# Four places for raw pieces of weights, and a new order of the first part, in a kernel of windowed attention and two products

## The chip, the core and the metric

The program runs on one core of a Trainium2 chip. The engines of a core are called by the names of its profile: PE (TensorE, matrix products; PEld is its loading of weights), DVE (VectorE), ACT (ScalarE), POOL (GpSimd) and SP (SyncE, which issues nearly all DMAs here). Each engine works through a queue of its own in order; semaphores tie the queues together. The metric is the device time of one execution in microseconds (us); lower is better.

## What is computed

The reference, cut to what matters (B = 4, H = 8, S = 768, D = 64; 8 global keys, a window of 96; 3072 tokens, d_model 512, d_ff 2048):

```
scores = q @ k.T / sqrt(D) - slope[h] * dist      # slope[h] = 2 ** -(h + 1)
keep   = key is among the first 8, or 0 <= query - key < 96
a      = softmax(where(keep, scores, -1e9))
x      = (a @ v), heads side by side              # 3072 x 512
h      = x @ w_in                                 # 3072 x 2048
g      = h if h >= 1;  0 if h <= -1;  else (h + 1) ** 2 / 4
out    = g @ w_out                                # 3072 x 512
```

The queries, keys and values are 32-bit floats, the two weights are 64-bit floats. The products have to be nearly as exact as in 32-bit arithmetic.

## The kernel before

*Tiling.* Work is cut into 24 units of 128 queries of one batch, all heads: units 0 to 3 are the first 128 queries of the four batches, units 4 to 23 the rest, batch by batch. Two units make a block `c` of 256 tokens, 0 to 11. Every operand of a large product is split into a high and a low half of 16 bits, and three products of halves (high x high, high x low, low x high) make one of nearly 32 bits.

*The first units* (`first_scores`, `masked`, `expo`, `first_turn`, `first_pt`, `first_av`, `scale_x`, `first_xt`, `first_x`) need only their own 128 keys and are computed in 32 bits, half a unit (four heads, `hf` 0 or 1) at a time. Their bias stands in `own_bias`, which lies over place 7 of the tile `wd`; a `slope` makes the bias of one head. The other units fetch k, q and v (`fetch`, on SP), convert them into halves (`conv_hi` on ACT, `conv_lo` mostly two steps on POOL, L767 and L768), put the 32 global keys ahead of the window (`keep_glob`, `set_glob`), and go through `scores`, `masked`, `expo`, `split_p`, `turn_p`, `attend`, `scale_x`, `split_x`, `turn_x`.

*Weights.* They come in 32 pieces `n` of 512 KB, 0 to 15 of w_in and 16 to 31 of w_out. `w_load` (SP) brings the raw 64-bit pieces into a place of `wd`: place `n % 3`. `w_bits` (DVE, L532, L536, L540; for the pieces marked "s" in `WS` the middle step is one of ACT, followed by `w_sign` on POOL) builds the 32-bit float out of two halves of 32 bits, in another part of `wd`, places 3 to 6. `w_hi` (ACT, L549) and `w_scale` (ACT, L560) make the high half and the scaled piece, and `w_lo` (POOL, L567) the low half. Steps 0 of pieces 5, 7, 9 and so on of w_in use the PSUM tile `spare(1)` ("spare" in the trace), the others a tile of the scores ("w_bits"). A raw place can be loaded again when the last step that reads it is over.

*The two products.* `ffn1(c, g)` (L939) is 24 matmuls for two of the 16 slices of d_ff and needs weight pieces 2g and 2g+1 and all four `x` steps of the block. `gelu(c, g, s)` is the nonlinearity: step 0 on ACT (L958), 1 and 2 on DVE (L962, L964), then, for blocks 0 to 2, step 3 on ACT and step 4 on POOL (L972), which make the halves `ga`. `ffn2(c, t, f)` (L998) is the product with w_out for blocks 0 to 2. For later blocks gelu has ten steps and the second product is done with seven products of sums and differences (`diff`, `first_products`, `last_products`, L1042), whose weight differences are kept in `wd` once its raw places are no longer wanted. `ffn1` has two PSUM tiles (`h`); gelu holds one until its step 2. The results of step 0 stand in one of three tiles `u`.

*Order.* All of this is a plan of 3311 items. The list `PLACE` gives the sequence in which they are emitted, and so the order in each engine's queue; `SLOTS` gives the tile that each takes among its like. Both are written out. Beside the items the list holds 37 fillers (`warm`, L494): matmuls of zeros into `spare(0)`. In the queue of PE the stretch from 30 to 75 us goes in pairs: `ffn1(1,g)`, then `ffn1(0,g')`, as fast as weights arrive. `scores(4)` and `scores(5)` follow near 99 and 105 us, and `ffn2` of block 0 behind them.

Of the kernel before, what the change touches and what calls it, by code (L numbers as in the profile page):

```python
# [24 lines left out]
NFC = DFF // P  # L25
# [256 lines left out]
    "v": [int(n, 16) for n in "012100201201212010201201"],  # L282
    "x": [int(n, 16) for n in "101001010110100110111001101011000110011010010110"],
    "xh": [int(n, 16) for n in "1010100101100110010101011010100110101001"],
    "xt": [int(n, 16) for n in "011010101010"],
    "z": [int(n, 16) for n in "101010101011010101001011001011001100101101001"],
}
NFILL = 200
# [53 lines left out]
def fast_path(ctx, tc, q, k, v, nraw, nval, w_in, w_out, out, half, one, stat, marks, badi):  # L342
# [37 lines left out]
    def after(*keys):  # L380
        assert did.issuperset(keys), keys
# [1101 lines left out]
```

## Time and profile before

| | us |
|---|---|
| median of 3 runs | 594.23 (592.88 to 594.45) |
| the profiled execution | 592.99 |
| its span in the trace | 591.1 |
| PE busy | 571.7 (97%) |
| POOL busy | 502.2 (85%) |
| DVE busy | 473.5 (80%) |
| ACT busy | 440.2 (74%) |

The span runs from the first to the last instruction of the trace; the execution's own time is 1.9 us more. The times of the trace below are microseconds from the start of the span. The granted clock of PE is full in every slice of the page.

### The profile page before, as it was taken

To read this page: it belongs to the slowest core of one execution; us is meant where nothing else is said; L and a number is where in the kernel's file an instruction comes from. 1 tells how busy PE (TensorE), PEld (TensorE's weight loads), DVE (VectorE), ACT (ScalarE), POOL (GpSimd) and SP (SyncE) were. 2 spreads that over 40 slices of the span, in tenths; PEclk is the share of its full clock that TensorE was granted. 3 is DMA by queue.
4 is the path that set the end of the run, shared out by engine and by line. 5 is a ranking of instruction groups with operands and counts; after the bars stand their busy time and mean duration, and the time that the engine had idled before them with its cause. 6 is when DMAs were issued, how large, how long until landed. Compare 5 with 4: busy or idle time off the path is not lost.

```text
span 591.1 us, 16452 instructions
## 1 busy us (share of the span) xinstructions
PE 571.7 (97%) x6243; PEld 475.7 (80%) x6243; DVE 473.5 (80%) x1175; ACT 440.2 (74%) x1146; POOL 502.2 (85%) x570
## 2 busy tenths in 40 slices
PE   7998999899999999999999999999999999999995
PEld 5876764457768688988888889888889889898884
DVE  8998999999884788787987987888979877874321
ACT  5998898998866798776976877868868768635340
POOL 0888999879999999899899998799899799579780
PEclk9999999999999999999999999999999999999999
DMA  7875675694840557848865777767667677250001
GB/s 248 279 247 189 203 238 185 144 173 88 191 105 2 114 129 153 179 127 197 196 160 129 171 176 155 179 172 188 169 150 170 158 172 171 56 123 1 2 37 42
DMA packets 144235, 88.19 MB, mean 149 GB/s; under 512 B 108180, under 2 KB 124820, under 8 KB 144148
## 3 DMA queue, kind: packets, MB, share of 16 engines
q1 hardware_dynamic: 144144, 87.05, 59.1%
q8 instruction: 51, 0.84, 0.6%
q14 instruction: 36, 0.29, 0.2%
q10 hardware_dynamic: 4, 0.00, 0.0%
HBM read 54.53 MB, written 6.29 MB: 103 GB/s over the span
## 4 chain that ended last, share of the span: by engine, by line
PE 66%; DVE 11%; ACT 10%; DMA 5%; POOL 4%; issue 3%; ACTq 0%; SPq 0%; DVEq 0%; POOLq 0%
PE h L939 30%; PE o L1042 26%; ACT z L644 5%; PE s L813 4%; PE av L854 4%; PE o L998 3%; DMA wd<-in_moe_w_out_dram 2%; DMA wd<-in_moe_w_in_dram 2%; DVE wd L540 2%; DVE u L964 1%; DVE h L962 1%; ACT ph L827 1%; POOL ga L972 1%; DVE w_bits L536 1%; DVE ph L829 1%
## 5 line engine op out<-in xcount | busy, mean ns | idle before, releaser
L939 PE MATMUL h<-xt,wih 128*128 128x256 f16 x1536 | 256.0, 273 | 5.0 <-DVE u L964 4.9
L939 PE MATMUL h<-xt,wil 128*128 128x256 f16 x768 | 209.3, 273 | 0.0
L939 PEld LDWEIGHTS <-wih 128*128 128x128 f16 x1536 | 148.4, 98 | 29.2 <-DVE u L964 9.9
L962 DVE SCALAR_TENSOR_TENSOR h<-h,u 128x512 f32<-128x512 f32 x96 | 66.4, 692 | 42.1 <-ACT u L958 41.6
L644 ACT ACTIVATE z<-z,stat 128x256 f32<-128x256 f32 (+1 forms) x192 | 91.5, 479 | 9.2 <-DVE stat L632 9.1
L983 POOL TENSOR_TENSOR ga<-u,ga 128x512 f16<-128x512 f32 x72 | 88.3, 1227 | 10.1 <-ACT ga L981 9.8
L1042 PEld LDWEIGHTS <-ga 128*128 128x128 f16 x864 | 83.2, 98 | 10.0
L958 ACT ACTIVATE u<-h,half 128x512 f32<-128x512 f32 x96 | 65.1, 678 | 33.0 <-PE h L939 22.6
L939 PEld LDWEIGHTS <-wil 128*128 128x128 f16 x768 | 75.2, 98 | 8.7
L974 POOL TENSOR_TENSOR u<-u 128x256 f32<-128x256 f32 x72 | 60.2, 838 | 20.0 <-DVE u L964 18.9
L988 POOL TENSOR_TENSOR gb<-u,gb 128x384 f16<-128x384 f32 x72 | 72.0, 1002 | 3.7 <-ACT gb L986 3.7
L1042 PE MATMUL o<-wd,ga 128*128 128x256 f16 x432 | 70.7, 273 | 0.0
L1042 PE MATMUL o<-woh,ga 128*128 128x256 f16 x288 | 70.7, 273 | 0.0
L1042 PEld LDWEIGHTS <-gb 128*128 128x128 f16 x648 | 62.3, 98 | 8.4 <-issue 1.0
L981 ACT ACTIVATE ga<-u 128x512 f16<-128x512 f32 x72 | 44.4, 621 | 33.2 <-POOL u L976 26.6
L964 DVE SCALAR_TENSOR_TENSOR u<-u,h 128x512 f32<-128x512 f32 x96 | 65.2, 680 | 3.6
L829 DVE SCALAR_TENSOR_TENSOR ph<-z,ph 128x1024 f16<-128x1024 f32 x40 | 57.0, 1428 | 9.4 <-ACT ph L827 9.0
L632 DVE CUSTOM_DVE_ANT_0 z<-s,bias 128x256 f32<-128x256 f32 x160 | 59.1, 414 | 5.1 <-PE s L813 4.7
L998 PE MATMUL o<-woh,ga 128*128 128x512 f16 x192 | 61.4, 379 | 0.6 <-ACT ob L1115 0.6
L1042 PE MATMUL o<-wd,gb 128*128 128x256 f16 x432 | 60.6, 273 | 0.8 <-DVE ob L1093 0.8
L998 PEld LDWEIGHTS <-ga 128*128 128x128 f16 x288 | 27.3, 98 | 30.6 <-issue 2.2
L599 DVE TENSOR_REDUCE stat<-c_raw 128x1 f32<-128x256 f32 x128 | 48.5, 406 | 4.3 <-DMA c_raw<-in_moe_w_in_dram 4.3
(132 smaller groups left out, 1172.2 us busy)
## 6 DMA issues: line engine op xcount, KB each, us to landing
wd<-in_moe_w_in_dram SPq DMA_DIRECT2D x16, 512.0 KB, 4.5
wd<-in_moe_w_out_dram SPq DMA_DIRECT2D x16, 512.0 KB, 4.2
c_raw<-in_moe_w_in_dram SPq DMA_DIRECT2D x32, 256.0 KB, 3.0
c_raw<-in_moe_w_out_dram SPq DMA_DIRECT2D x32, 256.0 KB, 3.4
kr<-in_k_dram SPq DMA_DIRECT2D x28, 256.0 KB, 3.6
vr<-in_v_dram SPq DMA_DIRECT2D x28, 256.0 KB, 3.6
qr<-in_q_dram SPq DMA_DIRECT2D x24, 256.0 KB, 3.9
out_dram<-ob SPq DMA_DIRECT2D x23, 256.0 KB, 3.1
```

Of the source, the lines that this page charges most:

```text
L632: nc.vector.tensor_tensor_reduce(out=p32[u, hf][:, hh, :], in0=pts[u, hf][hh // 2][:, hh % 2, 0:n], in1=(own_bias if n == P else bias)[:, ...
L644: nc.scalar.activation(z, z, AF.Exp, bias=nm[:, c : c + 1], scale=-1.0, accum_out=sums[:, c : c + 1])
L829: nc.vector.scalar_tensor_tensor(phs[u, hf][:, 1, :], zf, SP_, phs[u, hf][:, 0, :], op0=ALU.mult, op1=ALU.subtract)
L939: nc.tensor.matmul(hp[:, :, e, :], w[:, dc, f], xt[:, hf, 2 * a + j, :], start=(n == 0), stop=(n == 3 * NDC - 1),)
L958: nc.scalar.activation(u, h, AF.Relu, bias=half, scale=2.0 / (SV * SW), accum_out=su[:, col : col + 1])
L962: nc.vector.scalar_tensor_tensor(h, h, 4.0 / (SV * SW), u, op0=ALU.mult, op1=ALU.max)
L964: nc.vector.scalar_tensor_tensor(u, u, 4.0, h, op0=ALU.min, op1=ALU.mult)
L974: nc.gpsimd.tensor_sub(f[:, 3:7:3], f[:, 0:6:5], f[:, 4:5].to_broadcast([P, 2, P]))
L983: nc.gpsimd.tensor_sub(gas[c, g][:, 1], f[:, 0:4], gas[c, g][:, 0])
L988: nc.gpsimd.tensor_sub(gbs[c, g][:, 1, 0:3], f[:, 4:7], gbs[c, g][:, 0, 0:3])
L998: nc.tensor.matmul(po, a, w[:, f, :], start=(f == 0 and n == 0), stop=(f == NFC - 1 and n == 2))
L1042: nc.tensor.matmul(acc[:, e], x, w, start=first and n == 0, stop=last and n == 2)
```

## The change

Three constants are new (`R4`, `GM`, `WL`), the formula of the raw place in `w_load` is another, and `PLACE` and `SLOTS` are written anew. With the values given to `GM` and `WL`, the new branches in `w_lo`, `put_weight` and `gelu` (a gelu by squares, low halves made on DVE) are never taken, so they change nothing.

```
+R4 = 9
+GM = "d"
+WL = "pppppppppppppppppppppppppppppppp"
...
     def w_load(n):
         num, src, hi, lo = piece(n)
-        r = wd[:, n % 3].bitcast(I32).rearrange("p t a b -> p (t a b)")
+        r = wd[:, n % 3 if n < R4 else (7, 0, 1, 2)[(n - R4) % 4]].bitcast(I32).rearrange("p t a b -> p (t a b)")
...
     def w_lo(n):
-        after(("hi", n), ("scale", n))
-        nc.gpsimd.tensor_sub(lo, wf[n], hi)
         did.add(("w", n))
+        if WL[n] == "v":
...
+        else:
+            after(("hi", n), ("scale", n))
+            nc.gpsimd.tensor_sub(lo, wf[n], hi)
...
 PLACE = [
-    0, 2, 1, 10, 13, 8, 20, 11, 4, 29, 3, 5, 6, 7, 89, 90, 91, 31, 15, 21, 16, 19, 18, 14, 38, 30, 39, 43, 34, 41, 26,
...
```

Pieces 0 to 8 keep their places. Piece 9 goes to place 7, piece 10 to place 0, 11 to 1, 12 to 2, 13 to 7 and so on, each four behind the last one in its place; place 7 is that of the first units' bias.

The items are the same but for six fillers more (43). What changes in `PLACE` is their sequence. On each engine the last part of the queue is the same list before and after: the last 371 items of PE, 544 of DVE (from `split_x(10,0,1)`), 418 of ACT and 335 of POOL (from `gelu(4,0,.)`), 160 of SP. Before that, up to about 255 us of the old run, the sequence differs, mostly by a few positions. The queue of DVE from its 95th to its 121st step, old and new:

```
 95 gelu(0,1,1)          w_bits(9,0)
 96 w_bits(9,0)          w_bits(10,0)
 97 first_x(3,1,1)       first_x(3,1,1)
 98 w_bits(9,1)          w_bits(9,1)
 99 gelu(0,1,2)          gelu(0,1,1)
100 w_bits(9,2)          w_bits(9,2)
101 w_bits(10,0)         gelu(0,1,2)
102 w_bits(10,1)         w_bits(10,1)
103 w_bits(11,0)         w_bits(11,0)
104 w_bits(10,2)         w_bits(10,2)
105 gelu(1,0,1)          w_bits(12,0)
106 w_bits(11,2)         gelu(1,0,1)
107 gelu(1,0,2)          w_bits(12,1)
108 w_bits(12,0)         gelu(1,0,2)
109 gelu(0,2,1)          w_bits(11,2)
110 w_bits(12,1)         gelu(0,2,1)
111 gelu(0,2,2)          w_bits(12,2)
112 w_bits(13,0)         gelu(0,2,2)
113 w_bits(12,2)         w_bits(13,0)
114 w_bits(13,1)         w_bits(14,0)
115 gelu(1,1,1)          w_bits(13,1)
116 w_bits(13,2)         gelu(1,1,1)
117 gelu(1,1,2)          w_bits(13,2)
118 w_bits(14,0)         gelu(1,1,2)
119 gelu(0,3,1)          w_bits(14,2)
120 w_bits(14,2)         w_bits(16,0)
```

On SP the loads of pieces keep about their sequence among the fetches (`w_load(14)` and `w_load(16)` move ahead of a fetch, `fetch(4,"v",0)` moves back from the 25th to the 41st item). On POOL three `conv_lo` of units 4 and 5 move ahead of steps of weights. In the middle, the steps of blocks 1 and 2 and of units 6 to 9 are put in another sequence on all engines.

## Rows read from the trace of the kernel before

**Rows 1.** The page, part 1: busy time of an engine, share, instructions.

```profile
PE 571.7 (97%) x6243; PEld 475.7 (80%) x6243; DVE 473.5 (80%) x1175; ACT 440.2 (74%) x1146; POOL 502.2 (85%) x570
```

**Rows 2.** Windows: stretch, its us, engines' busy us (count), PEclk, DMA share, GB/s.

```profile
45.00:60.00 15.00, 12.75 (x106) 9.75 (x104) 13.19 (x23) 13.21 (x30) 13.16 (x13) 1.00 0.58 180
165.00:180.00 15.00, 15.00 (x140) 11.51 (x139) 11.59 (x18) 7.41 (x18) 14.82 (x16) 1.00 0.26 64
240.00:270.00 30.00, 30.00 (x346) 26.92 (x344) 24.99 (x60) 22.45 (x56) 27.16 (x32) 1.00 0.68 149
```

**Rows 3.** PE's timeline: start us, us, engine, line, operation, out<-in, count, [idle <-releaser].

```profile
37.27 0.38 PE L939 MATMUL h<-xt,wih 128*128 128x256 f16 x2
...
42.52 1.03 PE L494 MATMUL spare<-zeros 128*128 128x512 f16 x4
...
44.29 0.39 PE L939 MATMUL h<-xt,wih 128*128 128x256 f16 x2 [0.75 <-DVE u L964]
...
51.78 0.39 PE L939 MATMUL h<-xt,wih 128*128 128x256 f16 x2 [1.07 <-DVE u L964]
...
99.30 1.50 PE L813 MATMUL s<-kh,qh 64*128 64x128 f16 x47 [1.30 <-DVE wd L540]
...
105.43 1.51 PE L813 MATMUL s<-kh,qh 64*128 64x128 f16 x48 [0.53 <-DVE kh L795]
```

**Rows 4.** DVE's timeline, 31 to 97 us, columns as in the group before.

```profile
31.15 0.68 DVE L540 SCALAR_TENSOR_TENSOR wd<-wd,w_bits 128x512 int32<-128x512 int32 x1
...
36.39 0.68 DVE L532 TENSOR_SCALAR spare<-wd 128x512 int32<-128x512 int32 x1
...
39.80 0.70 DVE L532 TENSOR_SCALAR w_bits<-wd 128x512 int32<-128x512 int32 x1 [0.58 <-DMA wd<-in_moe_w_in_dram]
...
43.55 0.68 DVE L964 SCALAR_TENSOR_TENSOR u<-u,h 128x512 f32<-128x512 f32 x1
...
44.73 0.70 DVE L532 TENSOR_SCALAR w_bits<-wd 128x512 int32<-128x512 int32 x1 [0.50 <-DMA wd<-in_moe_w_in_dram]
...
48.05 0.69 DVE L532 TENSOR_SCALAR spare<-wd 128x512 int32<-128x512 int32 x1 [0.84 <-DMA wd<-in_moe_w_in_dram]
...
48.65 0.68 DVE L540 SCALAR_TENSOR_TENSOR wd<-wd,w_bits 128x512 int32<-128x512 int32 x1
...
96.17 0.69 DVE L532 TENSOR_SCALAR w_bits<-wd 128x512 int32<-128x512 int32 x1 [0.68 <-DMA wd<-in_moe_w_out_dram]
```

**Rows 5.** The chain of waits in order of time: start us, us, what.

```profile
42.47 5.55 DMA wd<-in_moe_w_in_dram
...
51.15 5.11 DMA wd<-in_moe_w_out_dram
...
168.24 2.62 PE h L939 x24
...
375.29 2.05 ACT z L644 x9
```

**Rows 6.** The page, part 6: DMAs, KB each, median us to landing.

```profile
wd<-in_moe_w_in_dram SPq DMA_DIRECT2D x16, 512.0 KB, 4.5
wd<-in_moe_w_out_dram SPq DMA_DIRECT2D x16, 512.0 KB, 4.2
...
kr<-in_k_dram SPq DMA_DIRECT2D x28, 256.0 KB, 3.6
```

**Rows 7.** POOL's timeline, its first weight step and two conversions.

```profile
15.50 1.16 POOL L567 TENSOR_TENSOR wil<-wd,wih 128x512 f16<-128x512 f32 x1 [14.65 <-ACT wd L560]
...
61.28 0.64 POOL L767 TENSOR_SCALAR kr<-kr 128x512 f32<-128x512 f32 x1
...
63.13 0.61 POOL L767 TENSOR_SCALAR kr<-kr 128x512 f32<-128x512 f32 x1
```

**Rows 8.** Timelines of ACT and of PE in the middle.

```profile
161.79 0.69 ACT L958 ACTIVATE u<-h,half 128x512 f32<-128x512 f32 x1 [2.46 <-POOL ga L972]
...
164.15 0.39 PE L939 MATMUL h<-xt,wih 128*128 128x256 f16 x2 [0.88 <-DVE u L964]
```

More of the change, by code (lines that the diff above doesn't have):

```diff
@@ L107 @@
 PLACE = [
[158 rows of a table removed]
[158 rows of a table added]
 ]
 SLOTS = {
-    "ga": [int(n, 16) for n in "b469a7318025bc4943c798b07251a839bc460ab7130259cb6a5704b6b1873a590642c8304bc7531a29b0652852b7a34c01698564a086b27c456a935b91745082ac7b62b3b715c62a8b490c3498132b6a0749c640"],
-    "h": [int(n, 16) for n in "11011010111010101010101010010101010101001101110101010010010101010110101010010110101010101010110100101010100"],
-    "in": [int(n, 16) for n in "13520432105435124013454021350215423105314352141054212541013012134231524535142052"],
-    "k": [int(n, 16) for n in "201201021020120120120120"],
@@ L272 @@
-    "kg": [int(n, 16) for n in "0000"],
-    "o": [int(n, 16) for n in "101001101010101001100101101001010110010110101"],
-    "ob": [int(n, 16) for n in "02102202001010021202010121100110"],
-    "ph": [int(n, 16) for n in "00011010101001010110101010100101010101011010"],
-    "pt": [int(n, 16) for n in "010110111010100101100101010110011001011001100110"],
-    "q": [int(n, 16) for n in "01010110100101010110"],
-    "r": [int(n, 16) for n in "011010100110110111011001011010100110100101010101"],
-    "raw": [int(n, 16) for n in "1001100110100110101011000110100011010010101100011010010011010100"],
@@ L280 @@
-    "s": [int(n, 16) for n in "0231213102031232131203120313120301233321330103101210120103212301303210331210320213312010201312231003012300102320321001012323213003321001031222012323230112021313210302123031302113021322"],
-    "u": [int(n, 16) for n in "21212012011201211202102100210202120102102011021020102102102102101201202120120120120102102021002021021021"],
-    "v": [int(n, 16) for n in "012100201201212010201201"],
-    "x": [int(n, 16) for n in "101001010110100110111001101011000110011010010110"],
@@ L284 @@
-    "xh": [int(n, 16) for n in "1010100101100110010101011010100110101001"],
-    "xt": [int(n, 16) for n in "011010101010"],
-    "z": [int(n, 16) for n in "101010101011010101001011001011001100101101001"],
+    "ga": [int(n, 16) for n in "74ca5836b019274ab5284a7096b28a5374b0185cb0638745a28b915a6c50b2879a5436593510cb8746a9524c2a307b465891c29359470ac632b1752028c37941a65c817b057421a609a20c3b2a870436c9125a3c"],
+    "h": [int(n, 16) for n in "01010100100101010101010101010101010101010101001010101010000101010101010101101110010101010110110100101001011"],
@@ new lines @@
+    "in": [int(n, 16) for n in "51230154302410352423514302143025150342351430113452101042325145540354234500301453"],
+    "k": [int(n, 16) for n in "201201201202121021021021"],
+    "kg": [int(n, 16) for n in "1111"],
+    "o": [int(n, 16) for n in "101010011010101001010101101010101001101001010"],
+    "ob": [int(n, 16) for n in "02012121010102120110201201101220"],
+    "ph": [int(n, 16) for n in "01111010101010011001011010100101100101100101"],
+    "pt": [int(n, 16) for n in "011011010101100110100110101010011110100110011001"],
@@ new lines @@
+    "q": [int(n, 16) for n in "01010010101010101001"],
+    "r": [int(n, 16) for n in "001111010111100110010110010101011010100110010101"],
+    "raw": [int(n, 16) for n in "1010011001011001011111010100100100101111010010010101010010010010"],
+    "s": [int(n, 16) for n in "3120312013120310230213213020321010323030201202120301212130213201201320113202311230023123023320021313013210312032310201230103310233203132201332130232213031013221123013102323023123032113"],
+    "u": [int(n, 16) for n in "20210102102012021220120212102121012021021200120101210210210120121021020120101201201210210120112120120210"],
@@ L287 @@
+    "v": [int(n, 16) for n in "012202102102102101201210"],
+    "x": [int(n, 16) for n in "111101011101100110011001010110110101101101101000"],
+    "xh": [int(n, 16) for n in "1010011010100110010110100110100101100110"],
+    "xt": [int(n, 16) for n in "100101010101"],
+    "z": [int(n, 16) for n in "101011010101010011001100101011001101010010110"],
 }
@@ L565, in w_lo @@
         num, src, hi, lo = piece(n)
-        after(("hi", n), ("scale", n))
-        nc.gpsimd.tensor_sub(lo, wf[n], hi)
         did.add(("w", n))
+        if WL[n] == "v":
+            after(("hi", n))
+            nc.vector.scalar_tensor_tensor(lo, wf[n], SW, hi, op0=ALU.mult, op1=ALU.subtract)
+        else:
+            after(("hi", n), ("scale", n))
+            nc.gpsimd.tensor_sub(lo, wf[n], hi)
     def put_weight(n, t, tl):
@@ L581, in put_weight @@
         at(t + WO[0], w_hi, n)
-        at(t + WO[1], w_scale, n)
+        if WL[n] != "v":
+            at(t + WO[1], w_scale, n)
         at(t + WO[2], w_lo, n)
@@ L946, in fast_path, with square @@
     gas, gbs = {}, {}
+    def square(c, g):
+        return GM[min(c * (NFC // 2) + g, len(GM) - 1)] == "s"
     def gelu(c, g, s):
-        after(("g", c, g, (None, 0, 1, 2, 3, 4, 4, 6, 5, 8)[s])) if s else None
+        after(("g", c, g, (None, 0, 10 if square(c, g) else 1, 2, 3, 4, 4, 6, 5, 8, 1)[s])) if s else None
         did.add(("g", c, g, s))
@@ L960, in gelu @@
             )
+        elif s == 1 and square(c, g):
+            nc.gpsimd.tensor_scalar(u, u, 4.0, 1.0, op0=ALU.min, op1=ALU.mult)
+        elif s == 10:
+            nc.scalar.activation(u, u, AF.Square)
+        elif s == 2 and square(c, g):
+            nc.vector.scalar_tensor_tensor(u, h, 16.0 / (SV * SW), u, op0=ALU.mult, op1=ALU.max)
         elif s == 1:
@@ L1160, in put_ffn1 @@
             at(t + GEL[s], gelu, c, g, s)
+            if s == 1 and square(c, g):
+                at(t + GEL[1] + 0.6, gelu, c, g, 10)
     def put_ffn2(c, ts, g, t):
```

315 rows, old and new, of the table PLACE are left out of this document.

## The prediction

> **What bounds the kernel now.** I read the page's busy shares first [rows 1]: TensorE (PE) is busy 97% of the 591.1 us span, so only time in which it waits, or works on fillers, can be won. The table of windows [rows 2] splits the run. From 165 us on PE is busy 15.00 us of 15, and the chain of waits [rows 5] is PE alone until 374. Before that PE has gaps; at 45 to 60 us it is down to 12.75 of 15, and VectorE (DVE, 13.19), ScalarE (ACT, 13.21) and GpSimd (POOL, 13.16) are all fuller. The change touches the order up to about 255 us, so the first 165 us decide.
>
> How PE loses there is seen in its timeline [rows 3]. The first-product steps of a pair of blocks, `ffn1(1,g)` and the next `ffn1(0,g')`, are 2.62 us each (24 matmuls, as the chain shows such steps), 5.24 for two. The pairs start at 37.27, 44.29 and 51.78, a fourth of the same kind at 59.41: 7.0, 7.5 and 7.6 us apart. The difference is filled with matmuls of zeros (L494) and a last wait of 0.75, 1.07 and, in the fourth, 1.00 us for DVE's L964, the second gelu step of an earlier `ffn1`, which frees the PSUM tile.
>
> DVE's timeline [rows 4] says what DVE did meanwhile. An operation of weights or gelu starts 0.60 us after the one before it (48.05 to 48.65). From the end of the gelu of (1,0) at 44.2 (L964, from 43.55) to that of (1,1) DVE has 10 of these in the old order, 6.0 us, and two waits for raw weights of 0.50 and 0.84: 7.3, against 7.5 seen. To that of (1,2) it has 11, 6.6 us, and one more such wait, 0.98: 7.6. So DVE sets the pace, and the raw loads add to it. Six such waits stand in its timeline (four of them in rows 4), for pieces 10, 12, 13, 16, 26 and 30: 0.58 + 0.50 + 0.84 + 0.98 + 0.36 + 0.68 = 3.94 us. Behind 97 us PE waits 1.30 at `scores(4)` and 0.53 at `scores(5)` [rows 3]; four more gaps of that kind follow, 0.59 at 107.86 for POOL's last weight, 0.58 at 109.68 for the output tile, and in the middle 0.46 and 0.88, the last in [rows 8].
>
> **Part 1, four places.** A load can be issued when the place's former piece has been read. In the old code that is piece n-3, in the new code, from piece 10 on, n-4. From issue to DVE's start the chain shows four pieces, 5.11 to 5.55 us, mean 5.33 [rows 5]; I take 5.3. A piece costs DVE two or three operations and the gelus between them, about 3.5 us, so the fourth place gives each load some 3.5 us more; that covers the old waits. But the new order uses this room: it takes several pieces earlier. I follow each tight load against the new list, in the old run's times:
> - Piece 10 still goes to place 0 and now needs piece 6 read, 32.3 us (L540 from 31.15 in rows 4, with 0.5 us more work before it). It lands at about 37.5. The new order puts its first step directly behind that of piece 9, at 36.6 (36.39 in rows 4, 0.6 less work ahead, 0.2 for a later start below, 0.60 for piece 9). DVE waits 0.9 where it waited 0.58, and `first_x(3,1,1)`, on which `ffn1(1,0)` depends, is now queued behind that wait: `ffn1(1,0)` comes about 1 us later.
> - Pieces 12 to 14: each lands 0 to 3 us ahead of its step. No wait.
> - Piece 16: its place is free after piece 12's last step, three operations past the gelu of (1,0), 45.1 + 1.8 = 46.9, so it lands at 52.2; DVE is there 11 operations past that gelu, at 51.7. Wait 0.5.
> - Pieces 15 and 18 need a sign step on POOL to be over; they land within 0.5 us of their steps. I put 0.3 for both. Piece 26: none.
> - Piece 30 has eleven short steps between the release (piece 26) and its own, 4.8 us against 5.3: 0.5.
> Sum 2.2, so 1.7 us of 3.94 are won. Bounds: nothing, if all landings are as tight as in the old order, and 3.9.
>
> The trace of before has no four places, and its loads take 5.1 to 5.6 us. The Trainium skill (DMA: Bandwidth & Descriptors, section "Anatomy of one DMA") gives a fit of 2.0 us plus bytes by 436 GB/s, for GpSimd-issued transfers, which would be an estimated 3.2 us for 512 KB. By that the 2.2 us would vanish too. These rows, on SP's queue, do not agree with it, so I don't use it.
>
> SP's queue is in order. Piece 9 now goes to place 7, which holds the first units' bias until `masked(3,1)` is over (near 30 us by its steps); the old issue, behind the read of piece 6, was at 31.9. Behind it stand pieces 10 to 12 and the loads of unit 4.
>
> **Part 2, the order up to the second product.** The same instructions run, so the work of an engine up to a point both orders share is equal, and only idle time can differ. Such a point on DVE is `set_glob(5,k)`: in both lists it is the 206th step, with the same 205 before it, and PE's `scores(5)` at 105.43 waits for it [rows 3]. So what DVE saves in waits, `scores(5)` gains. At the front the new order puts two slopes of bias (0.14 us each) behind the first masks, where DVE waits for PE anyway: no gain; the first exponential stays. ACT has 1.5 us more before piece 0's scaling, so POOL's first weight starts at about 16.9, not 15.5 [rows 7]; its later waits cover that. I charge DVE 0.2 for its start.
>
> Six more fillers (43 for 37) are 6 x 0.216 = 1.3 us (four take 1.03 with a last one of 0.38, rows 3). They stand before `ffn1(1,0)`, `(1,1)` and `(1,3)`, where PE waits for DVE; I cost them nothing. Uncovered they cost up to 1.3.
>
> POOL gets three conversions of units 4 and 5 (L767 and L768) ahead of weights it used to do first. At about 1.85 us each by their starts (61.28, 63.13, rows 7), and with gelus, the work ahead of piece 13's last step grows by 7.7 us, of piece 15's by 1.1, of piece 17's by 4.4. POOL has idled 22.1 us by then in the old run, most of it before its first weight [rows 7]; with the late start and the gaps filled I expect 18.5. Then piece 13 is ready at 65.2 (needed about 68.4), 15 at 69 (71.8), 17 at 75.2 (77.1). So it is covered, by 2 to 3 us.
>
> Sum for `scores(5)`: 1.7 - 0.2 = 1.5 us earlier.
>
> **Part 3, the middle.** PE's 0.88 us at 164.15 goes back to ACT, which waited 2.46 us for a `u` tile until POOL's `gelu(2,3,4)` was over [rows 8]. In the new POOL order that step stands in front of `gelu(2,2,4)` and a weight-difference step, with 2.3 us less work ahead of it; on DVE 2.4 and on ACT 2.7 us less stand ahead of the gelu of (2,4). The wait falls to near nothing, as does most of the 0.46 at 145. I take 1.1 us. Bounds: 0 (the next `u` tiles, of (2,6) and (2,7), get about 1 us tighter) and 2.5 (the 0.58 and 0.59 us go too).
>
> **Behind 165 us** PE is the chain, and what starts 2.6 us earlier stays so, if POOL follows. POOL is busy 27.2 us of 30 at 240 to 270 [rows 2]; it can.
>
> **Sum:** 1.5 + 1.1 = 2.6 us. The profiled run took 592.99 us, giving 590.4. The median of before is 594.23, 1.24 above that run; 2.6 off it gives 591.6, which I predict.
>
> **Rivals.**
> - *Loads land early.* If landing takes the DMA table's medians, 4.5 and 4.2 us [rows 6], all waits on raw weights go (3.9 - 0.2), and the middle gives 2.0: 594.23 - 5.7 = 588.5. Against: on the chain of this stretch they took over 5.1.
> - *POOL takes DVE's place.* If POOL has idled as much as before by 70 us (22.1), piece 17 is ready at 78.8, 1.7 us after PE wants it, and `u` tiles at 55 to 72 us are freed up to 1 us late. That eats the 1.5 and half of part 3: 593.6. For it: ACT and POOL are both over 13 of 15 busy [rows 2]. Against: most of POOL's gaps were waits for ACT.
> - *The lead is given back later.* At 374 to 412 us the chain leaves PE for ACT, POOL and DVE [rows 5]. If those queues do not move up, 594 again. Against: the chain enters them from PE's scores at 373, so they should shift too.
> - *SP's queue stalls ACT: slower.* The load of unit 4's second k block stands behind pieces 9 and 10 and needs `first_av(3,1)` over. ACT converts it right before `gelu(1,0)`, at 39.2. Issued by 33 it lands (3.6 us, rows 6) at 37 and nobody waits; issued at 35.0, the old end of `first_av(3,1)`, with 5.3 us it lands at 40.3, and ACT, POOL and through the gelu PE wait 1.1 us. From an issue at about 34 on it costs. With piece 10's 1 us before `ffn1(1,0)` and 1.3 us of fillers no longer hidden, and no load wait saved, that is 594.23 + 3.4 - 1.1 = 596.5.
>
> **How the numbers follow.** Forecast 0.40, loads land early 0.18, POOL 0.17, given back 0.08, SP 0.17. Within 0.3%, 1.8 us, is about what a measurement cannot tell from no change. The forecast's own spread (0 to 1.5 us either way) puts 0.28 of its 0.40 beyond that: faster 0.28 + 0.18 + 0.03 = 0.49, within 0.34, slower 0.17. The range leaves out the slower rival's end and the best corner (all loads and all of the middle): 588.3 to 595.3.
>
> **What would show it.** DVE's waits for raw weights at 35 to 97 us: 2.2 us in all, the largest before piece 10. `ffn1(1,0)` about 1 us later than 37.27, `scores(5)` 1.5 us earlier than 105.43. No wait of ACT over 1 us for a `u` tile near 160. The same work behind 255 us, moved up by 2.6 us. I am wrong if POOL's or ACT's waits grow at 39 to 80 us, or if `scores(5)` is early and the end is not.

## The result, and the profile after

The changed kernel is slower: a median of 597.64 us (596.09 to 600.01, 11 runs) beside 594.29 (592.04 to 595.53, 11 runs) for the kernel before on the same chip. The ratio is 1.0068 with an interval of 1.0049 to 1.0086, which is 2.9 to 5.1 us. The profiled execution took 596.09 us, its span is 594.2, so in the traces the difference is 3.1 us (591.1 before).

What the prediction called is mostly there. The first part of the page, answering [rows 1], gives nearly the same busy times, but PE's is 2.6 us more, 1.9 of it in the matmuls of zeros (43 of them, 12.85 us, for 37, 10.94):

```profile
PE 574.3 (97%) x6249; PEld 475.7 (80%) x6249; DVE 471.8 (79%) x1175; ACT 440.3 (74%) x1146; POOL 501.8 (84%) x570
```

The windows of [rows 2] in the trace after (columns as there):

```profile
45.00:60.00 15.00, 14.85 (x116) 10.82 (x115) 14.88 (x26) 13.71 (x31) 14.11 (x14) 1.00 0.73 219
165.00:180.00 15.00, 15.00 (x131) 11.02 (x130) 10.36 (x20) 10.39 (x24) 14.00 (x14) 1.00 0.62 141
240.00:270.00 30.00, 30.00 (x346) 26.82 (x345) 24.20 (x59) 23.05 (x59) 27.65 (x34) 1.00 0.69 155
```

From 45 to 60 us PE is busy 14.85 us for 12.75, DVE 14.88 for 13.19: the waits on raw weights have gone. DVE's timeline has only two left between 28 and 100 us, 1.27 us in all for 3.94 [rows 4]:

```profile
34.77 0.69 DVE L535 TENSOR_SCALAR w_bits<-wd 128x512 int32<-128x512 int32 x1 [0.58 <-DMA wd<-in_moe_w_in_dram]
38.94 0.69 DVE L535 TENSOR_SCALAR w_bits<-wd 128x512 int32<-128x512 int32 x1 [0.69 <-DMA wd<-in_moe_w_in_dram]
```

PE's timeline after, at the steps of [rows 3] and [rows 8] and where it lost time later (L947 is the old L939, L821 the old L813, L982 the old L964, L862 the second product of attention, old L854):

```profile
38.56 0.38 PE L947 MATMUL h<-xt,wih 128*128 128x256 f16 x2
...
103.28 1.51 PE L821 MATMUL s<-kh,qh 64*128 64x128 f16 x48
...
122.37 0.86 PE L862 MATMUL av<-vh,pt 128*128 128x64 f16 x24 [0.51 <-DVE vh L805]
...
142.73 1.51 PE L821 MATMUL s<-kh,qh 64*128 64x128 f16 x48 [0.90 <-DVE kh L803]
...
145.39 0.39 PE L947 MATMUL h<-xt,wih 128*128 128x256 f16 x2 [1.15 <-DVE u L982]
...
162.15 0.38 PE L947 MATMUL h<-xt,wih 128*128 128x256 f16 x2
...
278.52 0.88 PE L862 MATMUL av<-vh,pt 128*128 128x64 f16 x24 [0.73 <-DMA pt<-ph]
...
415.94 0.87 PE L862 MATMUL av<-vh,pt 128*128 128x64 f16 x24 [1.16 <-DMA pt<-ph]
```

To see where the lead went, compare the starts of steps that have the same matmul work ahead of them in both sequences. (`scores(5)` isn't quite such a step: it starts 2.15 us earlier, but one `ffn2` step of 0.65 us has moved from ahead of it to behind it, so its lead is 1.5.)

| step on PE | before | after | after minus before |
|---|---|---|---|
| `ffn1(1,0)` | 37.27 | 38.56 | +1.29 |
| `scores(6)` | 114.30 | 112.34 | -1.96 |
| `scores(8)` | 143.04 | 142.73 | -0.31 |
| `ffn1(2,2)` | 145.01 | 145.39 | +0.38 |
| `ffn1(3,7)` | 206.28 | 206.54 | +0.26 |
| `attend(12,1)` | 277.37 | 278.52 | +1.15 |
| `attend(18,0)` | 411.23 | 412.15 | +0.92 |
| `attend(18,1)` | 413.23 | 415.94 | +2.71 |
| end of the span | 591.1 | 594.2 | +3.1 |

So the lead of the front was spent between 115 and 146 us. By 167 us PE was 0.71 ahead once more, since the wait of 0.88 [rows 8] has gone, and between 180 and 192 us it lost 0.97 again, 0.59 of it in two waits for DVE (0.26 at 182.85 and 0.33 at 189.45); no experiment looks into that. Two more losses came on top, at 277 and at 415 us, in the part whose sequence is the old one. The experiments take these places one by one.

### The profile page after: what moved, and what is told of

Same layout as the page of the kernel before. It is cut to its first block, busy times and chain, and to the rows that moved or that the text cites. A ratio compares the mean times of both kernels' runs of the same rounds, so it can differ in the third digit from the quotient of the medians.

```text
span 594.2 us, 16476 instructions
## 1 busy us (share of the span) xinstructions
PE 574.3 (97%) x6249; PEld 475.7 (80%) x6249; DVE 471.8 (79%) x1175; ACT 440.3 (74%) x1146; POOL 501.8 (84%) x570
## 4 chain that ended last, share of the span: by engine, by line
PE 57%; POOL 14%; ACT 9%; DVE 9%; DMA 5%; issue 4%; SPq 0%; ACTq 0%; POOLq 0%; DVEq 0%
PE h L947 26%; PE o L1060 22%; PE s L821 3%; PE o L1016 3%; ACT z L652 3%; PE av L862 3%; POOL wd L1051 2%; DMA pt<-ph 2%; DMA wd<-in_moe_w_in_dram 2%; POOL ga L990 2%; POOL u L992 1%; POOL ga L1001 1%; ACT ph L835 1%; DVE wd L543 1%; POOL kh L776 1%
## 5 line engine op out<-in xcount | busy, mean ns | idle before, releaser
L947 PE MATMUL h<-xt,wih 128*128 128x256 f16 x1536 | 256.1, 273 | 2.8 <-DVE u L982 1.9
L947 PE MATMUL h<-xt,wil 128*128 128x256 f16 x768 | 209.5, 273 | 0.0
L947 PEld LDWEIGHTS <-wih 128*128 128x128 f16 x1536 | 148.4, 98 | 26.6 <-DVE u L982 5.6
L1001 POOL TENSOR_TENSOR ga<-u,ga 128x512 f16<-128x512 f32 x72 | 85.8, 1193 | 13.6 <-ACT ga L999 13.5
L1060 PEld LDWEIGHTS <-ga 128*128 128x128 f16 x864 | 82.9, 98 | 10.4 <-POOL ga L1001 0.3
L947 PEld LDWEIGHTS <-wil 128*128 128x128 f16 x768 | 75.0, 98 | 9.5 <-issue 0.7
L1006 POOL TENSOR_TENSOR gb<-u,gb 128x384 f16<-128x384 f32 x72 | 73.7, 1027 | 6.6 <-ACT gb L1004 6.5
L982 DVE SCALAR_TENSOR_TENSOR u<-u,h 128x512 f32<-128x512 f32 x96 | 65.0, 679 | 3.5 <-DVE h L980 0.5
L1004 ACT ACTIVATE gb<-u 128x384 f16<-128x384 f32 x72 | 36.5, 514 | 21.6 <-POOL u L996 10.8
```

The source lines that it names most:

```text
L947: nc.tensor.matmul(hp[:, :, e, :], w[:, dc, f], xt[:, hf, 2 * a + j, :], start=(n == 0), stop=(n == 3 * NDC - 1),)
L982: nc.vector.scalar_tensor_tensor(u, u, 4.0, h, op0=ALU.min, op1=ALU.mult)
L1001: nc.gpsimd.tensor_sub(gas[c, g][:, 1], f[:, 0:4], gas[c, g][:, 0])
L1006: nc.gpsimd.tensor_sub(gbs[c, g][:, 1, 0:3], f[:, 4:7], gbs[c, g][:, 0, 0:3])
L1060: nc.tensor.matmul(acc[:, e], x, w, start=first and n == 0, stop=last and n == 2)
```

## The experiments

Below, "lost" is PE's time up to a step less the matmul work ahead of it; it compares traces whose sequences differ. One trace of the same queue is not another to a tenth: in two executions of kernels that have the old queue up to 100 us PE stood 1.0 and 1.1 us ahead of the trace of before by then. Differences of under 1 us between two traces are therefore read beside the medians. The size of the front's lead is such a difference: over all traces, `scores(6)` starts at 113.2 to 114.3 us in the six with the old first part (mean 113.8) and at 112.0 to 113.2 in the nine with the new one and its fillers (mean 112.4). So the lead is real, but 1.4 us is a better figure for it than the 1.96 of the table.

### At 415 us: which tile a load was given

The queue of SP is the same there in both kernels, but `SLOTS["raw"]` is not. It gives each small load of raw weights for the check (`check_load`, into `c_raw`) one of two tiles, and in the new list `check_load(20,1)` gets the tile that the load just before it has filled. SP's queue, before and then after (start us, us of the issue; SPq is SP's sequencer):

```profile
401.92 2.81 SPq L836 DMA_TRANSPOSE pt<-ph  x1
404.84 0.53 SPq L594 DMA_DIRECT2D c_raw<-in_moe_w_out_dram  x1
405.47 2.97 SPq L836 DMA_TRANSPOSE pt<-ph  x1
```

```profile
403.77 0.33 SPq L602 DMA_DIRECT2D c_raw<-in_moe_w_out_dram  x1
404.19 2.91 SPq L844 DMA_TRANSPOSE pt<-ph  x1
409.26 0.33 SPq L602 DMA_DIRECT2D c_raw<-in_moe_w_out_dram  x1
409.69 2.85 SPq L844 DMA_TRANSPOSE pt<-ph  x1
```

Before, the load follows the transpose at once. After, the first transpose is issued by 407.10 and the load stands until 409.26, when DVE has reduced what was in its tile (DVE's `check_reduce` steps run from 408.49). Behind it stands `turn_p(18,1)`, for which `attend(18,1)` waits: the chain of waits after is

```profile
409.69 6.21 DMA pt<-ph
...
415.94 0.87 PE av L862 x24
```

Two runs moved the tiles alone, without a change of any queue. In the first, the changed kernel got the old tiles for these loads, in the second, the kernel before got the new ones from piece 9's check on (both lists differ in more loads than the one above):

```
-    "raw": ... "1010011001011001011111010100100100101111010010010101010010010010"
+    "raw": ... "0101100110100110100100100110100100101101010010011010101100101011"
```

> The kernel after, every queue in its own order; only the two tiles that take the weight checks' loads (c_raw) are dealt out as in the kernel before from check_load(20,1) and check_load(18,1) on, where after gives both a tile that has just been filled. Theory A (the tiles, not the order, cost the time late in the run): the 1.8 us that after loses against before at attend(18,1), near 415 us, and the 0.25 near 500 us are gone: 597.6 - 2.0 = 595.6 us; check_load(18,1) no longer waits for a check_reduce, and PE does not wait before attend(18,1). Theory B (the new order costs the time, the waits near 415 us are only where it shows): 597.6 us.

```
-    "raw": ... "1001100110100110101011000110100011010010101100011010010011010100"
+    "raw": ... "0110100110100110100000101011011011010000101101101010101101101101"
```

> The kernel before, every queue in its own order and with three places; only the two c_raw tiles are dealt out as in after, from check_load(9,1) on (near 310 us). Theory A: the wait of PE before attend(18,1) appears here too and the run takes 594.3 + 2.0 = 596.3 us. Theory B: 594.3 us, as no order is touched.

The changed kernel with the old tiles took 595.51 us, 1.0024 (1.0006 to 1.0041) of before; a second measurement of the changed kernel as it is gave 597.47, 1.0066 (1.0045 to 1.0086):

> The kernel after, unchanged, beside the others of this group. Theory A: ratio to before 1.005 to 1.0065, 3 to 3.9 us, and in its trace again about 1.7 us more lost than before near 415 us (attend(18,1)); the 0.85 us lost near 277 us at attend(12,1) needs no cause in the order and may be absent.

The kernel before with the new tiles took 594.37, 1.0023 (1.0002 to 1.0045): 1.4 us more than before by the ratio, 0.6 by the medians (593.77); less than the 2, with an interval that holds it. SP's queue of the two, first the changed kernel with old tiles, then the old with new tiles:

```profile
406.64 3.12 SPq L844 DMA_TRANSPOSE pt<-ph  x1
409.87 0.51 SPq L602 DMA_DIRECT2D c_raw<-in_moe_w_out_dram  x1
410.48 3.12 SPq L844 DMA_TRANSPOSE pt<-ph  x1
```

```profile
402.23 2.85 SPq L836 DMA_TRANSPOSE pt<-ph  x1
407.29 0.33 SPq L594 DMA_DIRECT2D c_raw<-in_moe_w_out_dram  x1
407.73 3.05 SPq L836 DMA_TRANSPOSE pt<-ph  x1
```

The gap in SP's queue goes with the tile, whatever the order. From `attend(18,0)` to `attend(18,1)`, at equal work, PE takes 1.8, 2.0 and 1.9 us more than before in three traces with the new tile (after, after again, old order with new tiles), and no more than before with the old tiles. So the tile costs about 2 us, by the traces and by the medians of the changed kernel (597.47 to 595.51, ratios 1.0066 and 1.0024), and that is about half of the slowdown.

### The front: does the new order win by itself?

One run took the new order and places up to 128 us only, and the old order and tiles behind; another did the reverse, the old order with three places up to 125 us and the new one from there on, with the old tiles of the check. Each is a `PLACE` spliced out of the two lists.

```
 PLACE = [
-    ...  the sequence after
+    ...  the sequence after up to norm(6,1), then the items left, in the sequence before
```

> Order and places of after up to about norm(6,1), near 128 us, then order and tiles of before. Theory A: at scores(5) to scores(7) after is ahead of before by 1.9 us in the traces, and before's middle and end keep that: 594.3 - 1.9 = 592.4 us. Theory B (the early lead is lost again wherever it meets the shared engines, as POOL and DVE have no room): 594.3 us or more.

```
 PLACE = [
-    ...  the sequence after
+    ...  the sequence before up to about 125 us, then the items left, in the sequence after
```

> Order of before with three places up to about 125 us, then the order of after, with before's c_raw tiles late in the run. Prediction's third part: the wait of 0.88 us before ffn1(2,6) goes and 1.1 us are won: 592.7 us. Theory D (POOL sets the pace in the middle in either order; the new one gives 0.88 back and adds waits of 0.5 at attend(5,0), 0.9 at scores(8), 0.7 more at ffn1(2,2)): no gain, 594 to 595 us.

The early order alone took 594.45 us, 1.0021 (1.0001 to 1.0040): no gain. By its trace it is 1.1 us ahead of before at `scores(7)` (at equal work) and 0.15 ahead from `scores(10)` to `attend(12,0)`, and at 277 us it loses 1.8 us more (below). The new middle alone took 593.78, 1.0012 (0.9992 to 1.0031), and loses 31.6 us in all where before loses 31.5. So the lead isn't eaten by the new middle order: the old one eats it as well. That felled my theory that the front's gain would show once the rest was left as it was.

### Places and order, one without the other

```
-        r = wd[:, n % 3].bitcast(I32).rearrange("p t a b -> p (t a b)")
+        r = wd[:, n % 3 if n < 12 else (7, 0, 1, 2)[(n - 12) % 4]].bitcast(I32).rearrange("p t a b -> p (t a b)")
```

> The kernel before, order and tiles untouched; from piece 12 on raw pieces go to places 7, 0, 1, 2 in turn, so that each may be loaded one piece earlier. The prediction's price list says that DVE's waits for pieces 12 to 30 (0.50 + 0.84 + 0.98 + 0.36 + 0.68 = 3.4 us) go, and that scores(5) comes that much earlier less what another engine holds back: 1 to 3 us. Theory D (POOL sets the pace from 135 to 250 us, and what DVE and PE win before does not reach it): the end moves by at most 0.5 us, 593.8 to 594.3 us.

```
-R4 = 9
+R4 = 99
```

> The kernel after with three places again (piece n in place n % 3); the issue of 17 loads stands a little later in SP's queue, behind the last read of the piece before in the place; the other queues are as in after. If the new order needs the fourth place, DVE waits for raw pieces 3 to 6 us more in all and scores(5) comes 2 to 5 us later than in after (103.3); the end is 599 to 602 us. Theory D: POOL takes up the first part of that delay, the end moves by less than half of what scores(5) loses.

In the second, 17 loads were also moved behind the last read of their place, since three places have no room for them earlier. The old order with four places took 594.29 us, 0.9999 (0.9983 to 1.0014): the place alone gives nothing. The new order with three places took 620.92, 1.0462 (1.0445 to 1.0480), over 18 us worse than I had allowed for: its DVE waits eleven times for raw weights, 23.7 us in all, up to 3.88 at a time, and `scores(5)` comes at about 126 us. The new order lives on the fourth place.

Why the place alone gives nothing is seen in DVE's waits of the first of these kernels, and in its chain:

```profile
41.06 0.70 DVE L532 TENSOR_SCALAR w_bits<-wd 128x512 int32<-128x512 int32 x1 [1.06 <-DMA wd<-in_moe_w_in_dram]
...
43.72 0.69 DVE L532 TENSOR_SCALAR spare<-wd 128x512 int32<-128x512 int32 x1 [1.23 <-DMA wd<-in_moe_w_in_dram]
```

```profile
37.37 6.32 DMA wd<-in_moe_w_in_dram
```

Only these two waits are left in place of six, 2.29 us for 3.94, but they are larger than the old ones: three loads of 512 KB are now in flight together (issued at 35.4, 37.4 and 37.8 us, landed at 41.0, 43.7 and 45.2), and they take 5.7, 6.3 and 7.4 us where the old chain showed 5.1 to 5.6 [rows 5]. A load that is issued earlier into a busy stretch doesn't land earlier by as much. (This profiled execution, 595.07 us, is the slowest of its twelve: PE waits 2.52 us at 46.85 and then runs at a lower clock for 3.4 us.)

### The middle: whose queue has no room

The lead is PE's and DVE's. POOL never had it: up to 150 us POOL is idle 29.7 us in the trace before, 30.0 after and 29.8 with the early order alone; its first weight step, which [rows 7] show at 15.50, starts at 17.39. The early-order kernel's `ffn1(2,6)` waits as in [rows 8], for a `u` tile behind POOL's low half:

```profile
161.64 0.69 ACT L970 ACTIVATE u<-h,half 128x512 f32<-128x512 f32 x1 [2.45 <-POOL ga L990]
```

```profile
164.00 0.39 PE L947 MATMUL h<-xt,wih 128*128 128x256 f16 x2 [0.89 <-DVE u L982]
```

To see whether POOL sets the end there, POOL does one step of 1.16 us (`gelu(2,1,4)`) twice, in the early-order kernel and in the kernel before; the second writes the same values again:

```
                 nc.gpsimd.tensor_sub(gl, u, gh)
+                if (c, g) == (2, 1):
+                    nc.gpsimd.tensor_sub(gl, u, gh)
```

> As e3 (new order up to 128 us, then before), and POOL does the step gelu(2,1,4) twice (1.2 us; the same values are written). Theory D (POOL sets the pace of the middle once PE comes early): scores(9) 1.2 us later than in e3 (190.4 start): 191.6. If POOL has room: 190.4 to 190.7.

> The kernel before, and POOL does the step gelu(2,1,4) twice. Theory D: scores(9), which starts at 190.5 in before, comes 1.2 us later there too. If PE and DVE set the pace of the middle in before, 0 to 0.6 us later.

In both, PE's wait at `ffn1(2,6)` grows to 2.00 us, by 1.11 and 1.12, nearly the whole step; here the early order, then the old:

```profile
165.41 0.39 PE L947 MATMUL h<-xt,wih 128*128 128x256 f16 x2 [2.00 <-DVE u L982]
```

```profile
164.14 0.39 PE L939 MATMUL h<-xt,wih 128*128 128x256 f16 x2 [2.00 <-DVE u L964]
```

The times are 598.35 us, 1.0080 (1.0048 to 1.0112), and 595.21, 1.0027 (1.0008 to 1.0047). By the measure that was set beforehand, the start of `scores(9)`, theory D came out in neither: with the early order it is 193.40 us, where 191.6 was expected (PE's clock fell behind the wait, see the last section), and in the old order 190.46, no later than before, as its rival had it. But that execution was 1.1 us ahead of before up to the wait, and the old order with the new tiles, which was as far ahead, starts `scores(9)` at 189.43; against that one the doubled step costs 1.0 us.

What the executions differ by says the same. In five traces with the old order in the middle and POOL's steps as they were, POOL has idled 28.8, 29.7, 29.8, 29.8 and 30.9 us up to 150 us, and at 169 us, at equal work, PE is 1.03 ahead of before, level with it (before itself), 0.15 ahead, 0.06 behind and 1.24 behind: PE stands where POOL stands, whichever first part ran. So up to 164 us POOL has no slack, in the old order nor with the early new one: what PE gains ahead of it is a longer wait there.

The other way round, two of POOL's steps in that stretch (`gelu(2,0,4)` and `gelu(2,1,4)`) go to DVE, in the early-order kernel, in the kernel before, and (with the old tiles and a move told below) in the changed kernel:

```
-                nc.gpsimd.tensor_sub(gl, u, gh)
+                (nc.vector if c == 2 and g < 2 else nc.gpsimd).tensor_sub(gl, u, gh)
```

> As e3 (new order up to 128 us, then before), but the low halves of two gelus of block 2, gelu(2,0,4) and gelu(2,1,4), are made by DVE instead of POOL (1.2 us each on POOL, about 0.7 on DVE). Theory D (POOL sets the pace at 135 to 190 us): POOL has 2.4 us less to do, the waits of 1.14 and 0.89 us before ffn1(2,2) and ffn1(2,6) shrink, and the run is 1 to 2 us faster than e3 (594.4): 592.4 to 593.4 us. If DVE sets the pace there, it is 1.4 us slower than e3: 595.8 us.

> The kernel before; the low halves of gelu(2,0,4) and gelu(2,1,4) on DVE instead of POOL, nothing else. Theory D (POOL sets the pace from 135 to 190 us in the old order too): the waits of 0.46 and 0.88 us before ffn1(2,2) and ffn1(2,6) go, PE is 1.1 to 1.3 us ahead of before at 190 us. If the middle waits for PE's or DVE's own work, it is 0 to 1.4 us behind.

> The kernel after with the c_raw tiles of e1, the two low halves of e8 on DVE and the two reductions of e9 moved. If the three places found are what cost the time, this run is ahead of before: 597.6 - 2.0 (tiles) - 1.5 (POOL, 1.15 + 0.26 us of waits in the middle) - up to 1 (check) = 593 to 594 us, 0 to 1 us ahead of before. If the new order costs time of its own in the middle, 595 us.

With the early order this works as far as 275 us: ACT's wait falls, the 0.89 goes, and PE is 1.3 us ahead of before at `scores(10)` and `attend(12,0)`, where the same kernel without the move is 0.15 ahead.

```profile
160.14 0.69 ACT L970 ACTIVATE u<-h,half 128x512 f32<-128x512 f32 x1 [0.88 <-POOL ga L990]
```

The time is 593.89 us, 1.0002 (0.9989 to 1.0015), since the lead is lost at 277 us. The kernel before gets 593.11, 0.9988 (0.9971 to 1.0006); in its trace `scores(9)` ends at 192.2 us, 192.0 without: the 0.88 has gone, but waits for DVE of 1.15 and 0.59 us have come at `ffn1(2,2)` and `ffn1(2,3)`, where DVE is the one that is late by its 1.4 us more. With the early order only the 0.59 is new there; a wait of 1.14 stood at `ffn1(2,2)` without the move too. In the changed kernel, 595.45 us, 1.0045 (1.0028 to 1.0062), the same two steps cost 1.6 us more in the middle (waits of 0.91, 1.15, 1.71 and 0.41 at `scores(8)` and the `ffn1` of block 2): in the sequence of its middle these steps of DVE come where PE waits for DVE already. Of the two times expected it is the higher one.

### At 277 us: a transpose behind loads and stores

At `attend(12,1)` PE waits 0.73 us after and not at all before, though all queues are the old ones from 255 us on. The chain there is `check_load(4,0)`, DVE's `check_reduce(4,0)`, `split_p(12,0,1)` behind it on DVE, then `turn_p(12,0)`, two more loads, two stores of the output and `turn_p(12,1)` on SP. The wait of DVE for the load is 0.72 us before, 1.13 after, 2.09 in the second trace of the changed kernel, 2.22 with the early order, and in the early-order kernel with low halves on DVE

```profile
263.96 0.42 DVE L607 TENSOR_REDUCE stat<-c_raw 128x1 f32<-128x256 f32 x1 [2.69 <-DMA c_raw<-in_moe_w_in_dram]
```

with a wait of PE of

```profile
278.39 1.34 PE L862 MATMUL av<-vh,pt 128*128 128x64 f16 x24 [2.06 <-DMA pt<-ph]
```

The traces show what the landing of that load goes with. One of the DMA queues on the page brings instructions in packets of 16 KB:

```profile
q8 instruction: 51, 0.84, 0.6%
```

By its pace it is PE's: a packet comes for about every 250 of PE's matmuls and weight loads. The twentieth comes near this load. In the eight traces of kernels with 37 fillers it starts 2.8 to 3.9 us after the load was issued, and the load lands after 2.9 to 3.3 us. In nine of the ten with 43 fillers it starts 1.1 to 2.3 us after the issue, in the middle of the load, and the load lands after 4.3 to 5.3; in the tenth, the trace after, it is 2.8 and 3.3. Counted in PE's own matmuls, fillers left out, the packet has 2472 to 2484 ahead of it with 37 fillers and 2460 to 2470 with 43: six fillers more in the same stream bring it earlier. Where the queues at 260 to 277 us are the old ones, PE waits before `attend(12,1)` in all seven traces with 43 fillers (0.73 to 2.06 us) and in none of the seven with 37. One of these seven is the changed kernel without six fillers (last experiment): its packet comes 3.6 us after the issue, and

```profile
263.24 0.42 DVE L607 TENSOR_REDUCE stat<-c_raw 128x1 f32<-128x256 f32 x1 [0.84 <-DMA c_raw<-in_moe_w_in_dram]
...
277.94 0.86 PE L862 MATMUL av<-vh,pt 128*128 128x64 f16 x24
```

So the loss at 277 us goes with the number of fillers and not with the order. That the packet itself delays the load is a reading of the traces; the kernel before with six fillers more was not run.

Two moves take the chain apart, on top of the early-order kernel with low halves on DVE: first two reductions of the check (items 1697 and 1728, `check_reduce(4,0,min)` and `check_reduce(4,1,max)`) go behind `split_p(12,0,1)` on DVE, then also the two stores `put_out(3,0)` and `put_out(3,1)` (items 1526 and 1529), ready since about 248 us, go to 258 us on SP, ahead of both `turn_p`. The last run makes both moves in the kernel before.

```
 PLACE = [
...
-    1581, 1545, 1577, 1551, 1572, 1697, 1629, 1605, 1579, 1728, 1614, 1599, 1608, 1592, 1611, 1610, 1621, 1612, 1731,
+    1581, 1545, 1577, 1551, 1572, 1629, 1605, 1579, 1614, 1599, 1608, 1592, 1697, 1728, 1611, 1610, 1621, 1612, 1731,
```

> As e8, and two reductions of the weight check, check_reduce(4,0) and (4,1), go behind split_p(12,0,1) in DVE's queue. In e8's trace PE was 1.2 us ahead of before at 255 us and lost 3.9 us at 277 to 285, after DVE had waited 2.69 us at check_reduce(4,0) for a load that took 4.9 us. Theory E (a housekeeping load that lands late stands in front of the softmax's split and eats the lead): with the wait out of the way the lead stays, 593.9 - 1.2 = 592.7 us, and DVE has no wait over 1 us ahead of split_p(12,0,1). Rival (the transposes on SP's queue set the pace there, whatever DVE does): 593.9 us.

```
 PLACE = [
...
-    ... 1593, 1553, 1567, 1564, 1565, ... 1706, 1637, 1526, 1529, ...
+    ... 1593, 1553, 1526, 1529, 1567, 1564, 1565, ... 1706, 1637, ...
```

> As e9, and put_out(3,0) and (3,1) are issued behind turn_x(11,0), near 258 us, not between the two transposes of unit 12, near 268 us. Theory F (transfers in flight slow the transpose that PE waits for): turn_p(12,1) takes less than e9's 4.2 us on SP and lands before PE wants it; the 0.98 us wait before attend(12,1) goes, and the lead of 1.1 us lasts to the end: ratio 0.998, 592.3 us. Rival (the transpose takes that long by itself, as it writes 512 KB): as e9, 593.3 us.

> The kernel before with the two moves of e9 and e13 alone (reductions of the check behind split_p(12,0,1), outputs of block 3 behind turn_x(11,0)). In the profiled execution of before no wait stands at 277 us, but in other executions of the same tail 0.7 to 4 us do; if that is chance that hits before too, the median falls by 0.5 to 1 us: ratio 0.9985. If before is not hit: 1.000.

The first move gives 593.26 us, 0.9996 (0.9978 to 1.0013); PE still waits 0.98 us, since the transpose behind the stores takes long to issue. With the stores moved, it doesn't: SP's queue with the stores in the old place, and with them moved,

```profile
268.30 0.93 SPq L1141 DMA_DIRECT2D out_dram<-ob  x2
269.33 4.18 SPq L844 DMA_TRANSPOSE pt<-ph  x1
```

```profile
258.09 1.05 SPq L1141 DMA_DIRECT2D out_dram<-ob  x2
...
269.07 2.94 SPq L844 DMA_TRANSPOSE pt<-ph  x1
```

PE's wait is gone, and the kernel takes 592.32 us (591.61 to 593.08) beside 593.92, 0.9976 (0.9964 to 0.9989): the fastest of all, faster than both kernels of this case by more than the interval. The kernel before with the same two moves takes 593.71, 1.0002 (0.9987 to 1.0018): no wait stood there, so there was nothing to win. So with the new first part and room given to POOL, DVE and SP behind it, 1.6 us come out at the end (in the two profiled executions 0.5, 590.6 for 591.1, as that of before is one of its faster ones). That they are the front's alone is not shown: the old order with all three changes was not run, and with the low halves on DVE alone it stood at 0.9988.

### The six fillers

```
 PLACE = [
-    ... 318, 329, 96, 97, 327, 308, 337, 341, 320, 724, 331, 328, 350, 98, 99, 326, ...
+    ... 318, 329, 327, 308, 337, 341, 320, 724, 331, 328, 350, 326, ...
```

> The kernel after without the six fillers that stand between 19.0 and 21.6 us of its trace. By that time after is 1.4 us behind before. Theory A: the delay at the front is made up for by 95 us anyway, since DVE and ACT set the pace there: 597.6 us. Theory C (uncovered fillers are lost for good, the slower rival's last term): 1.3 us less, 596.3 us.

Without the six (items 96 to 101, at 19.0 to 21.6 us) the changed kernel took 596.08 us, 1.0037 (1.0018 to 1.0056). These are not the ones that the new order added: ahead of 36 us it has 16 fillers where the old one has 17, and the added ones stand behind. `ffn1(0,0)` starts at 25.07 us for 25.30: PE waits where it worked on zeros. By 95 us the two traces have lost the same, so where they stand the six cost nothing. The medians say 1.4 to 1.6 us, with intervals that overlap, and the traces have a place for that: at 277 us PE loses nothing without the six, and 0.9, 1.5 and 2.1 us in the three traces of the changed kernel's queues with them (after, after again, old tiles), where the packet of instructions falls into the load. At the end the traces have lost 34.7 us without the fillers and 34.5 with, as the first was later by 0.3 us ahead of 255 us and lost 0.4 us more at 415; a single trace against a single trace doesn't show the difference that the medians do.

## Why the prediction was wrong

I predicted 591.6, 588.3 to 595.3, and gave slower 0.17; it is slower, above the range. The last sign of being wrong that I had named is the one that came: `scores(5)` is early and the end is not. By the prediction's own steps:

- **Part 1, the loads: right, the gain under-sized.** 1.27 us of waits are left where I had 2.2: 0.69 before piece 10 (predicted 0.9), none at pieces 16, 26 and 30, and one I hadn't seen, 0.58 at piece 8. `first_x(3,1,1)` and `ffn1(1,0)` behind piece 10 are late by 1.29 us (predicted about 1), but that is luck: the six traces with the old first part reach `ffn1(1,0)` at 37.3 to 38.8 us, mean 38.0, the nine with the new one at 38.0 to 39.1, mean 38.5.
- **Part 2, up to the second product: right.** `scores(5)` is 1.5 us ahead at equal work, as summed; to the tenth that is luck too, as the means of the same traces (104.9 and 103.4) give 0.9. I told its start as 1.5 us earlier; it is 2.15, because an `ffn2` step of 0.65 changed sides on PE, which I hadn't looked for. POOL's first weight comes at 17.39 (predicted 16.9), and POOL covers it. (Its idle time by 70 to 77 us of the old run is 21.7 to 21.8 us, not 22.1.)
- **Part 3, the middle: the named wait goes, the sum fails.** `ffn1(2,6)` at 162.15 has no wait, as forecast. But I counted the waits that go and looked for no new ones. From `scores(6)` to `ffn1(2,2)` PE waits 0.51, 0.90 and 1.15 us after, where it waited 0.46 before: 2.1 us, which is nearly the 2.34 by which the lead turns into +0.38. Of the waits for a `u` tile near 160 I said none over 1 us; one of 1.62 stands at 171.74, and costs PE nothing.
- **"What starts earlier stays so, if POOL follows; it can."** This step is the first that failed, and the row under it was the wrong one. POOL's 27.2 of 30 us busy at 240 to 270 [rows 2] says nothing about 105 to 165 us, where POOL decides; [rows 2] show it at 14.82 of 15 just behind. The doubled step showed no slack there (1.11 and 1.12 us of wait for 1.16 of work), with two steps taken from POOL PE was 1.3 us ahead to 275 us, and PE's place at 169 us follows POOL's idle time trace by trace. The two rivals that said so, POOL in DVE's place (593.6) and a lead given back later (594), named the mechanism, too early and too late; neither ends slower.
- **"The same work behind 255 us, moved up by 2.6 us": failed twice.** The diff changes `SLOTS` for the whole run. I had written that the last part of each queue is the same list, and took the tiles for part of the front. The new tiles of `SLOTS["raw"]` cost about 2 us at 415. And a queue that is the same isn't the same in time: the load at 260 us, whose landing varied from 2.9 to 5.3 us between traces, decides what PE waits at 277.
- **"Six more fillers ... I cost them nothing": wrong, by a path that the prediction hasn't.** I asked only whether PE has room for them where they stand. With 43 fillers PE waits at 277 us in seven traces of seven, with 37 in none of seven; in the changed kernel that is 0.9 us (1.5 and 2.1 in two other traces of its queues), and the medians without six of them are 1.4 to 1.6 us lower.
- **The slower rival (SP's queue stalls ACT near 39 us) wasn't the cause** (ACT waits 0.17 and 0.25 us for k, at 36.89 and 40.26 us, where the rival had 1.1), though it ended nearest, at 596.5, and though SP's queue it was, 375 us later.

In sum, by the traces: 1.5 us won to `scores(5)` and 0.46 behind it, 2.22 given back by 207 us (2.34, 1.09 of it won back, then 0.97 lost), 0.89 lost at 277, 0.23 won on the way to 411, 1.79 lost at 415 and 0.4 behind: 3.1 us. The medians differ by 3.35, and by the ratio 4.0.

## What to carry to other kernels

When a planned order is written anew, compare the tile of every step too, to the end of the program: a load that is given the tile just filled stands in its issuing queue until that is read, and all that is queued behind it stands too. A gain on one engine is worth as much as the slack of the next-fullest engine in the stretch where the two meet; read the busy share there, and test it by doing one of its steps twice. And count new waits as carefully as the one that is removed. A step that costs nothing where it stands, such as a filler, can still shift what comes later, so compare several executions with it and without it.

## What the runs showed of the hardware

*Transfers in flight slow one another, and the issue of a transpose.* Loads of 512 KB land after 4.5 and 4.2 us in the median before [rows 6] and took 5.1 to 5.6 on the chain [rows 5]; three in flight together took 5.7, 6.3 and 7.4. On SP the issue of the transpose `turn_p(12,1)` took 3.8 to 4.5 us in the sixteen traces where it stands right behind two stores, and 2.94 and 2.80 in the two with the stores moved away.

*Instruction packets and data loads.* A load of 256 KB landed after 2.9 to 3.3 us where a packet of PE's instructions (16 KB, mostly 0.9 to 1.0 us of a DMA engine's time) came 2.8 us or more after the load's issue, and after 4.3 to 5.3 us where it came 1.1 to 2.3 us after it; the eighteen traces have no exception.

*A wait holds the issuing queue.* The Trainium skill (DMA: Bandwidth & Descriptors, section "Anatomy of one DMA") states that DMA engines don't wait on semaphores and that such a wait happens on the issuing sequencer, before the transfer is handed over. The trace agrees: SP stands from 407.10 to 409.26 us, and the transpose behind it, whose data are ready, stands with it.

*PE's clock after waits of about 2 us.* In the early-order kernel with POOL's step doubled the granted clock is full up to the wait of 2.00 us at 163.4 to 165.4 and, from 165.7 to 169.1 us, at its lower level, 1.2 of 2.4 GHz (windows, columns as in [rows 2]):

```profile
163.00:165.00 2.00, 0.41 (x2) 0.00 (x0) 1.03 (x2) 1.95 (x6) 2.00 (x4) 1.00 0.98 212
...
166.00:169.00 3.00, 3.00 (x16) 2.06 (x15) 2.97 (x6) 1.69 (x5) 2.78 (x4) 0.50 0.34 74
```

`scores(9)` there ends 3.1 us later than without the doubled step: 0.3 us was lost before the wait, the wait grew by 1.11, and the slow stretch costs the other 1.7. The same fall, to 0.50, followed waits of 2.52 (old order, four places), 2.06 and 1.94 us in three other traces, each the slowest execution measured of its kernel, and of 3.76, 3.89 and 2.63 us in the new order with three places. It did not follow one of 2.72 there, one of 2.00 in the kernel before with POOL's step doubled, nor any of 1.88 or less after the first 10 us. So a wait of about 2 us can cost nearly twice what it shows; which of them do, these runs don't tell.
